# Windowed attention and a hard-swish MLP on one core: an order written by hand for all engines, and transposes moved from TensorE to the DMA engines

## The chip, the cores and the metric

The kernel runs on one core of a Trainium2 chip. A core has TensorE (PE; matmuls and transposes, reading SBUF and writing PSUM), VectorE (DVE), ScalarE (ACT), GpSimd (POOL) and SyncE (SP), which computes nothing and here issues most of the DMAs. Each engine runs its own instructions in order and waits on semaphores for the others. All DMAs share 16 DMA engines. The metric is the device time of one execution in microseconds, the median over several runs; lower is better.

## The reference

```python
q, k, v: (8 batches, 8 heads, 576 positions, 64) f32
scores = q @ k^T / 8;  kept where 0 <= i - j < 64, else -1e9
attn   = softmax(scores) @ v
x      = attn as (4608 tokens, 512)          # token = batch * 576 + position
h      = x @ w_in                            # w_in  (512, 2048)
g      = h * clip(h + 3, 0, 6) / 6
out    = g @ w_out                           # w_out (2048, 512), out (4608, 512) f32
```

The attention is narrow: a query sees 64 keys, so a block of 128 keys meets only 192 queries. The MLP does most of the arithmetic: in tiles of 128 x 128 weights against 512 columns it is 2 x 576 = 1152 matmuls.

## The kernel before

All matmuls take bf16; softmax is done without subtracting the maximum. Two heads together (64 + 64 features) fill 128 partitions and are called a pair; a batch has four pairs. There are nine token blocks T of 512 tokens, which don't coincide with the eight batches of 576.

**Loads.** `load_batch` (lines 67 to 85) brings one batch: q and k in runs of 1536 bytes (six positions of a head, 96 partitions), v in rows of 256 bytes (one position of a head), all issued by SP. The weights come by four plus four DMAs of GpSimd that cast to bf16 on the way (L94, L101). `cast_batch` (L160 to L166) makes bf16 copies; for batch 0 VectorE and ScalarE do it pair by pair, later GpSimd does.

**Attention** for a pair, in `attention`: `tq` (L178) transposes q and k on TensorE, 2 x 6 transposes of 96 x 96, and VectorE and ScalarE copy them out of PSUM, undoing the interleaving. `scores` (L201) computes key-by-query scores in 10 matmuls, ScalarE takes the exponential (L208, L214), VectorE multiplies with the mask (L219). `pv` (L231, L236) multiplies with V in 18 matmuls; a column of ones in V gives the sums, VectorE divides (L242, L245). `xt` (L255) transposes the result on TensorE in five transposes and ScalarE copies it (L260) into xT, features by tokens.

**MLP.** `s1(T)` computes 16 tiles hT (features of w_in by 512 tokens, 4 matmuls each, L280); ScalarE and VectorE make g of them (L285, L286). `s2(T)` multiplies g with w_out into acc, 16 matmuls for each of four groups of 128 tokens (L296); ScalarE copies acc out (L303) and SP stores it (L305).

**Order.** Attention of batch 0 stands alone. After that `weave` runs s1(T) zipped with s2(T-1) and puts the 24 pieces of attention of batch T+1 between them, up to T = 6; T = 7 and 8 have no attention, and s2(8) ends the kernel alone. The framework keeps this order for the engines and places the semaphores. PSUM is given out as one buffer each for transposes, scores, o and acc, and two for hT.

Of the kernel before, what the change touches and what calls it, by code (L numbers as in the profile page):

```python
# [22 lines left out]
def kernel(  # L23
# [15 lines left out]
    assert D == 64 and NG * P == DM and WINDOW == D  # L39
    KB = (S + P - 1) // P  # L40
    SP = KB * P
    R = 6
    NP = S // R
# [3 lines left out]
    assert NTB * TB == NT and NP * R == S  # L47
# [5 lines left out]
    stage = ctx.enter_context(tc.tile_pool(name="stage", bufs=1))  # L53
    nat = ctx.enter_context(tc.tile_pool(name="nat", bufs=2))
    small = ctx.enter_context(tc.tile_pool(name="small", bufs=4))
    opool = ctx.enter_context(tc.tile_pool(name="opool", bufs=2))
    gpool = ctx.enter_context(tc.tile_pool(name="gT", bufs=2))
    t1pool = ctx.enter_context(tc.tile_pool(name="t1", bufs=3))
    osbp = ctx.enter_context(tc.tile_pool(name="osb", bufs=3))
    ps_tr = ctx.enter_context(tc.tile_pool(name="ps_tr", bufs=1, space=PSUM))  # L60
    ps_st = ctx.enter_context(tc.tile_pool(name="ps_st", bufs=1, space=PSUM))
    ps_o = ctx.enter_context(tc.tile_pool(name="ps_o", bufs=1, space=PSUM))
    ps_h = ctx.enter_context(tc.tile_pool(name="ps_h", bufs=2, space=PSUM))
    ps_acc = ctx.enter_context(tc.tile_pool(name="ps_acc", bufs=1, space=PSUM))


    def load_batch(b, by_pair):
        qst = stage.tile([P, H, R * D], F32, name="qst", tag="qst")
        kst = stage.tile([P, H, R * D], F32, name="kst", tag="kst")
        vst = stage.tile([P, KB, H, D], F32, name="vst", tag="vst")  # L70
        step = 2 if by_pair else H
        for h0 in range(0, H, step):
            for dst, src in ((qst, q), (kst, k)):
                nc.sync.dma_start(
                    out=dst[:NP, h0 : h0 + step, :],
                    in_=src[b, h0 : h0 + step].rearrange("h (p j) d -> p h (j d)", j=R),
                )
        for kb in range(KB):
            s0 = kb * P
            ss = min(P, S - s0)  # L80
            nc.sync.dma_start(  # L81
                out=vst[:ss, kb, :, :],
                in_=v[b, :, s0 : s0 + ss, :].rearrange("h s d -> s h d"),
            )
        return qst, kst, vst

    stage0 = load_batch(0, True)


    win16 = consts.tile([P, NG, FF], BF16, name="win16")  # L90
    wout16 = consts.tile([P, NFC, DM], BF16, name="wout16")
    WC = FF // 4
    for i in range(4):
        nc.gpsimd.dma_start(  # L94
            out=win16[:, :, i * WC : (i + 1) * WC],
            in_=moe_w_in[:, i * WC : (i + 1) * WC].rearrange("(g p) f -> p g f", p=P),
        )

    def load_w_out():
        for i in range(0, NFC, 4):  # L100
            nc.gpsimd.dma_start(  # L101
                out=wout16[:, i : i + 4, :],
                in_=moe_w_out[i * P : (i + 4) * P, :].rearrange("(c p) j -> p c j", p=P),
            )


    ident32 = consts.tile([P, P], F32, name="ident32")
    make_identity(nc, ident32)
    ident = consts.tile([P, P], BF16, name="ident")
    nc.vector.tensor_copy(out=ident[:], in_=ident32[:])  # L110
    mask32 = consts.tile([P, QW], F32, name="mask32")
    nc.gpsimd.memset(mask32[:], 1.0)
    nc.gpsimd.affine_select(
        out=mask32[:], in_=mask32[:], pattern=[[1, QW]], compare_op=ISGE,
# [3 lines left out]
        out=mask32[:], in_=mask32[:], pattern=[[-1, QW]], compare_op=ISGE,  # L118
        fill=0.0, base=WINDOW - 1, channel_multiplier=1,
    )  # L120
    mask = consts.tile([P, 2 * KB, QW], BF16, name="mask")
    nc.vector.tensor_copy(
        out=mask[:], in_=mask32[:].unsqueeze(1).to_broadcast([P, 2 * KB, QW])
# [3 lines left out]


    NQT, NPT, NV = 3, 3, 2
    QT_ring, KT_ring, P_ring, V_ring = [], [], [], []  # L130
    for i in range(NQT):
        for ring, n in ((QT_ring, "QT"), (KT_ring, "KT")):
            t = consts.tile([P, SP], BF16, name=f"{n}{i}")
            nc.vector.memset(t[:, S:SP], 0.0)
            ring.append(t)
    for i in range(NPT):
        t = consts.tile([P, 2, KB, 2 * P], BF16, name=f"pT{i}")
        nc.gpsimd.memset(t[:], 0.0)
        P_ring.append(t)
    for i in range(NV):  # L140
        t = consts.tile([P, KB, H, VW], BF16, name=f"V{i}")
        nc.gpsimd.memset(t[:, :, :, D:VW], 1.0)
        nc.gpsimd.memset(t[D:P, KB - 1, :, 0:D], 0.0)
        V_ring.append(t)

    xT = consts.tile([P, NG, NT], BF16, name="xT")


    def cast_batch(b, st, first):
        qst, kst, vst = st  # L150
        qn = nat.tile([P, R, H, D], BF16, name="qn")
        kn = nat.tile([P, R, H, D], BF16, name="kn")
        V = V_ring[b % NV]
        step = 2 if first else H
        for h0 in range(0, H, step):
            for i, (n, s) in enumerate(((qn, qst), (kn, kst))):
                o_ap = n[:NP, :, h0 : h0 + step, :].rearrange("p j h d -> p h j d")
                i_ap = s[:NP, h0 : h0 + step, :].rearrange("p h (j d) -> p h j d", j=R)
                if not first:
                    nc.gpsimd.tensor_copy(out=o_ap, in_=i_ap)  # L160
                elif i == 0:
                    nc.vector.tensor_copy(out=o_ap, in_=i_ap)
                else:
                    nc.scalar.copy(out=o_ap, in_=i_ap)
        nc.gpsimd.tensor_copy(out=V[:, 0 : KB - 1, :, 0:D], in_=vst[:, 0 : KB - 1, :, :])
        nc.gpsimd.tensor_copy(out=V[0:D, KB - 1, :, 0:D], in_=vst[0:D, KB - 1, :, :])  # L166
        return qn, kn, V


    def attention(b, cast):  # L170
        st8 = {}

        def tq(g):
            c = cast()
            for n, (src, ring) in enumerate(((c[0], QT_ring), (c[1], KT_ring))):
                tr = ps_tr.tile([P, 1024], BF16, name="tr")
                for j in range(R):
                    nc.tensor.transpose(  # L178
                        out=tr[:, j * NP : (j + 1) * NP],
                        in_=src[:NP, j, 2 * g : 2 * g + 2, :].rearrange("p h d -> p (h d)"),  # L180
                        identity=ident[:NP, :NP],
                    )
                T = ring[(b * NG + g) % NQT]
                o_ap = T[:, 0:S].rearrange("d (p j) -> d p j", j=R)
                i_ap = tr[:, 0:S].rearrange("d (j p) -> d p j", p=NP)
                if n == 0:
                    nc.vector.tensor_copy(out=o_ap, in_=i_ap)  # L187
                else:
                    nc.scalar.copy(out=o_ap, in_=i_ap)
                yield  # L190

        def scores(g):
            QT, KT = QT_ring[(b * NG + g) % NQT], KT_ring[(b * NG + g) % NQT]
            pT = P_ring[(b * NG + g) % NPT]
            for kbs in ((0, 1), (2, 3, 4)):
                st = ps_st.tile([P, 2, 512], F32, name="st")
                off = 0
                for kb in kbs:
                    w = min(QW, SP - kb * P)
                    for h in range(2):  # L200
                        nc.tensor.matmul(  # L201
                            st[:, h, off : off + w],
                            lhsT=KT[h * D : (h + 1) * D, kb * P : (kb + 1) * P],
                            rhs=QT[h * D : (h + 1) * D, kb * P : kb * P + w],
                            start=True, stop=True,
                        )
                    off += w
                nc.scalar.activation(  # L208
                    out=pT[:, :, kbs[0] : kbs[0] + 2, 0:QW],
                    in_=st[:, :, 0 : 2 * QW].rearrange("p h (k w) -> p h k w", k=2),  # L210
                    func=EXP, scale=scale,
                )
                if len(kbs) == 3:
                    nc.scalar.activation(  # L214
                        out=pT[:, :, 4, 0:P], in_=st[:, :, 2 * QW : 2 * QW + P],
                        func=EXP, scale=scale,
                    )
                yield
            nc.vector.tensor_tensor(  # L219
                out=pT[:, :, :, 0:QW], in0=pT[:, :, :, 0:QW],  # L220
                in1=mask[:].rearrange("p (h k) w -> p h k w", h=2), op=MULT,
            )

        def pv(g):
            V = cast()[2]
            pT = P_ring[(b * NG + g) % NPT]
# [64 lines left out]
    def s2(T):  # L291
        gT = gTs[T]
        for ts in range(TB // P):
            acc = ps_acc.tile([P, DM], F32, name="acc")
            for fc in range(NFC):
# [4 lines left out]
                if fc % 4 == 3 and fc < NFC - 1:  # L300
                    yield
# [81 lines left out]
```

## Time and profile before

| | us |
|---|---|
| median of three runs (375.29, 375.0, 375.18) | 375.18 |
| span of the profiled execution, first to last instruction | 372.6 |
| TensorE busy with matmuls | 333.0 |
| ScalarE / VectorE / GpSimd busy | 214.6 / 194.6 / 74.7 |
| first matmul with w_in | 35.35 |
| the longest group: 512-column matmuls with w_in, 545 recorded | 152.2 |
| the next: 512-column matmuls with w_out, 559 recorded | 146.4 |
| 384 transposes of q and k on TensorE | 29.7 |
| 160 transposes of x on TensorE | 15.5 |

The profile names groups by line of the kernel, engine, operation and tile. Matmuls overlap each other, so the busy time of one is longer than the time by which it delays the next; starts tell more than lengths. A few per cent of the matmuls are not recorded (545 of 576). The DMA share is the busy part of the 16 DMA engines, and can go above 1 where packets overlap. The DMA engines moved 42.34 MB at a mean of 114 GB/s, nearly all loads in the first half.

### The profile page before, as it was taken

How to read it: one execution, taken by the hardware profiler on the slowest of the kernel's cores; microseconds unless marked ns; L12 is line 12 of the kernel's file. 1: busy time of each engine (PE TensorE's matmuls, PEld its weight loads, DVE VectorE, ACT ScalarE, POOL GpSimd, SP SyncE). 2: the span in 40 equal slices, each digit the busy share in tenths (PEclk: the TensorE clock that was granted, in tenths of full speed). 3: DMA queues.
4: the chain of work that ended last, by engine and by line, in shares of the span. 5: the costliest groups of instructions: out<-in, count | busy, mean ns of one | idle time of the engine just before them, and what ended most of it. 6: DMA issues, size and time to landing. Idle time of an engine off the chain costs nothing.

```text
span 372.6 us, 6265 instructions
## 1 busy us (share of the span) xinstructions
PE 333.0 (89%) x2544; PEld 168.6 (45%) x2592; DVE 194.6 (52%) x285; ACT 214.6 (58%) x345; POOL 74.7 (20%) x54
## 2 busy tenths in 40 slices
PE   0156789999999999999999999999999999999985
PEld 0134434555545455455545554555445444444432
DVE  2444438865674567466746665656565643343300
ACT  2353358857666666766676667666766644544411
POOL 8505523544511051005200520000000000000000
PEclk9999999999999999999999999999999999999999
DMA  8999999999999148605760000000000010110111
GB/s 189 248 209 239 196 210 222 218 203 237 199 251 224 42 128 184 157 28 138 173 156 31 28 31 28 30 30 28 30 28 31 29 56 28 45 41 28 57 57 56
DMA packets 59676, 42.34 MB, mean 114 GB/s; under 512 B 38656, under 2 KB 55040, under 8 KB 59648
## 3 DMA queue, kind: packets, MB, share of 16 engines
q1 hardware_dynamic: 55424, 37.76, 43.2%
q0 software_dynamic: 4224, 4.19, 6.8%
q8 instruction: 20, 0.33, 0.4%
q14 instruction: 8, 0.07, 0.1%
HBM read 36.70 MB, written 9.44 MB: 124 GB/s over the span
## 4 chain that ended last, share of the span: by engine, by line
PE 51%; ACT 2%; DVE 2%; DMA 1%; another core or an unknown queue 1%; issue 1%; SPq 1%; ACTq 0%
PE acc L296 23%; PE hT L280 20%; PE st L201 2%; PE tr L178 2%; DMA vst<-in_v_dram 1%; PE o L231 1%; PE tr L255 1%; PE o L236 1%; ACT osb L303 1%; DVE pT_145 L219 1%; ACT pT_145 L208 0%; SPq L81 0%; DVE QT_131 L187 0%; DVE pT_147 L219 0%
## 5 line engine op out<-in xcount | busy, mean ns | idle before, releaser
L280 PE MATMUL hT<-xT,win_110 128*128 128x512 bf16 x545 | 152.2, 386 | 3.7 <-ACT xT L260 1.8
L296 PE MATMUL acc<-wout_111,gT 128*128 128x512 bf16 x559 | 146.4, 379 | 3.7 <-ACT osb L303 3.0
L280 PEld LDWEIGHTS <-win_110 128*128 128x128 bf16 x576 | 52.5, 99 | 58.2 <-issue 4.7
L296 PEld LDWEIGHTS <-gT 128*128 128x128 bf16 x576 | 50.6, 98 | 52.8 <-issue 6.3
L160 POOL CAST qn<-qst 96x3072 bf16<-96x3072 f32 x7 | 19.4, 2778 | 74.4 <-issue 56.9
L303 ACT COPY osb<-acc 128x512 f32<-128x512 f32 x36 | 21.6, 601 | 16.3 <-PE acc L296 12.6
L178 PE MATMUL tr<-ident,qn 96*128 96x96 bf16 x192 | 14.9, 219 | 16.7 <-DVE ident L110 15.8
L245 DVE TENSOR_TENSOR opg<-o,rec 128x640 bf16<-128x640 f32 x32 | 26.4, 825 | 1.1
L260 ACT COPY xT<-tr 128x576 bf16<-128x576 bf16 x32 | 20.6, 642 | 9.0 <-PE tr L255 8.5
L178 PEld LDWEIGHTS <-qn 96*128 96x128 bf16 x192 | 12.8, 105 | 25.2 <-issue 14.0
L208 ACT ACTIVATE pT_147<-st 128x768 bf16<-128x768 f32 x20 | 16.1, 808 | 11.5 <-PE st L201 11.5
L208 ACT ACTIVATE pT_143<-st 128x768 bf16<-128x768 f32 x22 | 17.8, 808 | 7.1 <-PE st L201 7.1
L208 ACT ACTIVATE pT_145<-st 128x768 bf16<-128x768 f32 x22 | 17.7, 806 | 5.5 <-PE st L201 5.5
L160 POOL CAST kn<-kst 96x3072 bf16<-96x3072 f32 x7 | 19.2, 2740 | 6.6 <-DMA kst<-in_k_dram 6.6
L219 DVE TENSOR_TENSOR pT_143<-pT_143,mask 128x1920 bf16<-128x1920 bf16 x11 | 13.2, 1199 | 9.8 <-ACT pT_143 L214 9.8
L219 DVE TENSOR_TENSOR pT_145<-pT_145,mask 128x1920 bf16<-128x1920 bf16 x11 | 13.2, 1196 | 9.5 <-ACT pT_145 L214 9.5
L178 PEld LDWEIGHTS <-kn 96*128 96x128 bf16 x192 | 12.8, 105 | 11.1 <-issue 5.9
L178 PE MATMUL tr<-ident,kn 96*128 96x96 bf16 x192 | 14.8, 219 | 3.0 <-DVE QT_135 L187 1.3
L255 PE MATMUL tr<-ident,opg 128*128 128x128 bf16 x160 | 15.5, 231 | 2.0 <-DVE opg L245 1.2
L219 DVE TENSOR_TENSOR pT_147<-pT_147,mask 128x1920 bf16<-128x1920 bf16 x10 | 12.5, 1253 | 8.5 <-ACT pT_147 L214 8.5
L255 PEld LDWEIGHTS <-opg 128*128 128x128 bf16 x160 | 11.4, 102 | 10.6 <-DVE opg L245 4.4
L242 DVE RECIPROCAL rec<-o 128x10 f32<-128x10 f32 x32 | 6.9, 217 | 10.6 <-PE o L236 10.6
(355 smaller groups left out, 429.7 us busy)
## 6 DMA issues: line engine op xcount, KB each, us to landing
out_dram<-osb SPq DMA_DIRECT2D x36, 256.0 KB, 2.0
vst<-in_v_dram SPq DMA_DIRECT2D x32, 256.0 KB, 7.6
qst<-in_q_dram SPq DMA_DIRECT2D x6, 1152.0 KB, 9.2
kst<-in_k_dram SPq DMA_DIRECT2D x6, 1152.0 KB, 12.8
qst<-in_q_dram SPq DMA_DIRECT2D x8, 288.0 KB, 7.7
kst<-in_k_dram SPq DMA_DIRECT2D x8, 288.0 KB, 8.5
win_110<-in_moe_w_in_dram POOLq DMA_DIRECT2D x4, 512.0 KB, 15.2
wout_111<-in_moe_w_out_dram POOLq DMA_DIRECT2D x4, 512.0 KB, 15.0
```

The source lines that it names most:

```text
L160: nc.gpsimd.tensor_copy(out=o_ap, in_=i_ap)
L178: nc.tensor.transpose(out=tr[:, j * NP : (j + 1) * NP], in_=src[:NP, j, 2 * g : 2 * g + 2, :].rearrange("p h d -> p (h d)"), identity=iden ...
L201: nc.tensor.matmul(st[:, h, off : off + w], lhsT=KT[h * D : (h + 1) * D, kb * P : (kb + 1) * P], rhs=QT[h * D : (h + 1) * D, kb * P : kb * ...
L208: nc.scalar.activation(out=pT[:, :, kbs[0] : kbs[0] + 2, 0:QW], in_=st[:, :, 0 : 2 * QW].rearrange("p h (k w) -> p h k w", k=2), func=EXP, ...
L219: nc.vector.tensor_tensor(out=pT[:, :, :, 0:QW], in0=pT[:, :, :, 0:QW], in1=mask[:].rearrange("p (h k) w -> p h k w", h=2), op=MULT,)
L242: nc.vector.reciprocal(out=rec[:].unsqueeze(3), in_=ov[:, :, :, D:VW])
L245: nc.vector.tensor_tensor(out=opg[:].rearrange("p k h d -> p h k d"), in0=ov[:, :, :, 0:D], in1=rec[:].unsqueeze(3).to_broadcast([P, 2, KB ...
L255: nc.tensor.transpose(out=tr[:, qb * P : (qb + 1) * P], in_=opg[:, qb, :, :].rearrange("p h d -> p (h d)"), identity=ident[:],)
L260: nc.scalar.copy(out=xT[:, g, b * S : (b + 1) * S], in_=tr[:, 0:S])
L280: nc.tensor.matmul(hT[:], lhsT=win16[:, g, fc * P : (fc + 1) * P], rhs=xT[:, g, t0 : t0 + TB], start=(g == 0), stop=(g == NG - 1),)
L296: nc.tensor.matmul(acc[:], lhsT=gT[:, fc, ts * P : (ts + 1) * P], rhs=wout16[:, fc, :], start=(fc == 0), stop=(fc == NFC - 1),)
L303: nc.scalar.copy(out=osb[:], in_=acc[:])
```

## The change

The program is rewritten in one piece. The framework's own ordering is switched off (`manual_schedule`): each engine gets its instructions in the order in which the program writes them, and semaphores are still placed by the framework.

- **Weights** come as f32 by plain DMAs from SP through a staging ring of four buffers (`load_win`, `load_wout`), and GpSimd casts them.
- **Batches 0 and 1** (`load_qk_long`): q and k in runs of 2304 bytes (nine positions), so that two heads fill 128 partitions; one set of nine 128 x 128 transposes on TensorE (`tp_long`) serves two pairs, and the halves are copied out by VectorE and ScalarE. v of these two is issued by ScalarE. x of these two is transposed on TensorE as before.
- **Batches 2 to 7**: q in runs of 1024 bytes (four positions), k and v in rows of 256 bytes, all by SP. GpSimd casts them, and then SP issues DMA transposes from SBUF to SBUF: two for k, two for q per batch (`tk`, `tq`). x is transposed by DMA too, one per pair and block of 128 queries, more where a token block ends inside (`xt_dma`): 20 to 24 per batch. The queries stand in permuted order inside blocks of 64, so the mask and the stores follow that order, and a store of 128 tokens becomes two.
- **Order**: attention 0, s1(0), s2(0) by quarters of w_out (`s2_first`), attention 1 alone; then for T = 1 to 8 s1(T), and s2(T) with attention of batch T+1 in between (scores of pair g after 10g matmuls, pv after 16 + 10g). s1 and s2 are no longer zipped. At the top of each T SP gets the transposes of batch T+1 and then the loads of batch T+2.
- **PSUM**: three buffers of two banks for everything but acc, two for acc. The activation and the product of the MLP take two hT tiles at once (128 x 1024). gT has one buffer instead of two, the last scores of a pair are 64 columns wide instead of 128.

```diff
-    def load_batch(b, by_pair):
...
+    ctx.enter_context(tc.manual_schedule())
+    def load_qk_long(b, gg):
+        st = stage()
+        sv = st[:, 0 : 4 * S].rearrange("p (c a f) -> p c a f", c=2, a=2)
+        for c, src in ((0, q), (1, k)):
+            for a in range(2):
+                h0 = 4 * gg + 2 * a
+                nc.sync.dma_start(
+                    out=sv[:, c, a, :],
+                    in_=src[b, h0 : h0 + 2].rearrange("h (p j) d -> (h p) (j d)", j=J9),
+                )
+        return sv
...
+    qk0 = [load_qk_long(0, 0), load_qk_long(0, 1)]
+    v0 = load_rows(nc.scalar, v, 0)
...
+    def tq(n, t):
+        QT = qkt.tile([P, 4, NG, QJ], BF16, name="QT", tag="QT")
+        o = QT[:].rearrange("d j g p -> d (j g) p")
+        nc.sync.dma_start_transpose(out=o[:, :, 0:P], in_=n[:].rearrange("p j h d -> p (j h d)"))
+        nc.sync.dma_start_transpose(
+            out=o[:, :, P:QJ], in_=t[:].rearrange("p j h d -> p (j h d)")
+        )
+        return QT
+
+    def tk(n):
+        KT = qkt.tile([P, KB, NG, P], BF16, name="KT", tag="KT")
+        nc.gpsimd.memset(KT[:, KB - 1, :, D:P], 0.0)
+        nc.sync.dma_start_transpose(
+            out=KT[:, 0 : KB - 1].rearrange("d k g p -> d (k g) p"),
+            in_=n[:, 0 : KB - 1].rearrange("p k h d -> p (k h d)"),
+        )
+        nc.sync.dma_start_transpose(
+            out=KT[:, KB - 1, :, 0:D], in_=n[0:D, KB - 1].rearrange("p h d -> p (h d)")
+        )
+        return KT
+
+    def xt_dma(b, g, opg):
+        for qb in range(KB):
+            n = P if qb < KB - 1 else D
+            for T, o, f, c in xparts(b, qb * P, n):
+                nc.sync.dma_start_transpose(
+                    out=xtile(T)[:, g, o : o + c], in_=opg[f : f + c, qb, :]
+                )
...
+    def s1(T):
+        gT = gpool.tile([P, NFC, TB], BF16, name="gT", tag="gT")
+        x = xtile(T)
+        for c in range(0, NFC, 2):
+            hT = big()
+            for i in range(2):
+                for g in range(NG):
+                    nc.tensor.matmul(
+                        hT[:, i, :], lhsT=win16[:, g, (c + i) * P : (c + i + 1) * P],
+                        rhs=x[:, g, :], start=(g == 0), stop=(g == NG - 1),
+                    )
...
+            nc.scalar.activation(
+                out=t1[:], in_=hT[:], func=RELU, bias=half[:], scale=1.0 / 6.0
+            )
+            nc.vector.scalar_tensor_tensor(
+                out=gT[:, c : c + 2, :], in0=t1[:], scalar=1.0, in1=hT[:], op0=MIN, op1=MULT,
+            )
...
+    nat_cast(0, 0, qk0[0], (D_, A_, D_, A_))
+    win_st = [load_win(0)]
+    nat_tp(0, 0, 0, (D_, A_))
+    nat_tp(0, 0, 1, (D_, A_))
+    nat_cast(0, 1, qk0[1], (G_, D_, G_, D_))
+    nat_s(0, 0)
...
+    drive(s1(0), {})
+    v1 = load_rows(nc.scalar, v, 1)
...
+    for T in range(1, NTB):
+        b = T + 1
+        side = {}
+        if b < B:
+            cast_perm(b)
+            tr_perm(b)
+            if b + 1 < B:
+                pend[b + 1] = (
+                    load_q4(b + 1), load_rows(nc.sync, k, b + 1), load_rows(nc.sync, v, b + 1)
+                )
+            for g in range(NG):
+                side.setdefault(10 * g, []).append(lambda g=g: perm_s(b, g))
+                side.setdefault(16 + 10 * g, []).append(lambda g=g: perm_pv(b, g))
+        drive(s1(T), {})
+        drive(s2(T), side)
```

## The prediction

> **What bounds the kernel now.** I read the busy shares first, then the stages, then TensorE's own timeline, then the queue of the SyncE sequencer (SP).
>
> The page's first part, and busy time by stage (each row: stretch in us, its length, then busy us and instruction count for each engine, granted clock, DMA share, GB/s):
>
> ```profile
> PE 333.0 (89%) x2544; PEld 168.6 (45%) x2592; DVE 194.6 (52%) x285; ACT 214.6 (58%) x345; POOL 74.7 (20%) x54
> ...
> 0.00:35.30 35.30, 11.20 (x113) 7.97 (x115) 12.72 (x23) 11.80 (x17) 19.10 (x26) 1.00 1.07 221
> 35.30:73.00 37.70, 31.93 (x275) 16.82 (x279) 23.78 (x33) 23.73 (x40) 15.34 (x7) 1.00 1.14 212
> ...
> 258.00:295.00 37.00, 36.54 (x305) 18.63 (x310) 22.17 (x33) 24.52 (x40) 0.00 (x0) 1.00 0.08 30
> 295.00:352.00 57.00, 56.56 (x262) 25.64 (x266) 22.84 (x34) 28.04 (x43) 0.00 (x0) 1.00 0.10 38
> 352.00:372.60 20.60, 14.24 (x63) 6.14 (x63) 0.40 (x1) 2.78 (x5) 0.00 (x0) 1.00 0.17 64
> ```
>
> The kernel has two characters. Until some 75 us the DMA share is above 1 and TensorE is mostly waiting; after that TensorE has no idle time until the last stage. So time can be won at the start by bringing data sooner, and later only by giving TensorE less to do. The clock is 1.00 everywhere.
>
> TensorE's timeline inside a steady stage (start us, length us, line, operation, count), and at the end:
>
> ```profile
> 223.63 0.42 PE L178 MATMUL tr<-ident,qn 96*128 96x96 bf16 x6
> 223.89 1.03 PE L296 MATMUL acc<-wout_111,gT 128*128 128x512 bf16 x4
> ...
> 222.04 0.45 PE L255 MATMUL tr<-ident,opg 128*128 128x128 bf16 x5
> 222.33 0.59 PE L296 MATMUL acc<-wout_111,gT 128*128 128x512 bf16 x2
> ...
> 352.49 3.61 PE L296 MATMUL acc<-wout_111,gT 128*128 128x512 bf16 x16 [0.67 <-ACT osb L303]
> ```
>
> Sixteen 512-column matmuls take 3.61 us, the last of them 0.38, so one follows another in (3.61-0.38)/15 = 0.215 us; 64 of them, half a token block, take 13.8 us. Six q or k transposes delay the matmul behind them by 0.26 us (223.63 to 223.89), five x transposes by 0.29.
>
> SP's timeline, the v loads' issues (min/median/max ns), the store's and q's:
>
> ```profile
> 5.86 17.89 SPq L81 DMA_DIRECT2D vst<-in_v_dram  x5
> ...
> 122.25 9.72 SPq L305 DMA_DIRECT2D out_dram<-osb  x2
> ...
> 150.93 4.25 SPq L81 DMA_DIRECT2D vst<-in_v_dram  x4
> 159.04 9.72 SPq L305 DMA_DIRECT2D out_dram<-osb  x2
> ...
> L81 SPq DMA_DIRECT2D vst<-in_v_dram x40: 373/1082/7316, 5.9 to 190.9; - x40
> ...
> L305 SPq DMA_DIRECT2D out_dram<-osb x36: 332/333/4677, 86.1 to 369.7; - x36
> ...
> L74 SPq DMA_DIRECT2D qst<-in_q_dram x14: 340/450/1080, 0.8 to 171.6; - x14
> ```
>
> Stores of the same place in two stages lie 159.04-122.25 = 36.8 us apart: that is a stage, 128 matmuls (27.6 us) and 9.2 us of attention. A load in 256-byte runs holds the sequencer for as long as its data is moving: 17.89 us for five when the DMA engines are full, about 1.06 us each when they are not.
>
> **The start, until block 1 begins.** Before: first w_in matmul at 35.35 us, and block 0 with batch 1 woven in runs to about 77 us, because batch 1's v is cast only at 53.50 us. After: the order is attention 0, s1(0), s2(0), attention 1, with nothing woven in but two transposes.
> - First transposes at 12 us (before: 15.78, waiting for ident). The q and k of two pairs must land and be cast by VectorE and ScalarE; before, a first, smaller q is cast at 3.94 us. But ScalarE now issues the five v loads ahead of its casts. Nothing held: about 7 us. Held like SP's five: 18. I take 12, the middle, since the queue is ScalarE's own but the engines are full.
> - Attention 0 alone: 16.5 us. Before it runs from 15.78 to 35.35 with a 3.06 us wait for V inside: 19.57-3.06 = 16.5. ScalarE's sum supports it: 2 casts of 1.2 (0.83 x 1.5), 4 half evictions of 0.64, 4 pairs of exponentials of 1.9, 4 x copies of 0.9 are 16 us. s1(0) starts at 28.5.
> - s1(0) and s2(0): 2 x 13.8, to 56. Its cover is the data: 15.5 MB of weights and two batches must be in shortly after. They arrive at 235 GB/s as q and k do in the trace (66 us, so 10 late) or at 385, as a store's 2048-byte rows do in the window 357 to 358 (154 GB/s at a DMA share of 0.40; 40 us, not late). The new runs of 2048 and 2304 bytes on all 128 partitions are nearer the store's, v's are not: I take 2 us late. The casts of the weights go to GpSimd: 8 x 1.89 us (its 128x2048 cast) = 15 us, beside TensorE; GpSimd was busy only 20%. Without that cover each would delay a quarter of w_in by 1.9.
> - Attention 1 alone: 16.5 less the first pair's transposes and casts, which lie in s2(0): 13 us. Block 1 starts at 28.5+27.6+2+13 = 71 us, where before it started at about 77 with s2(0) and its 13.8 us still to do.
>
> **Blocks 1 to 6**, each with one batch. Removed: 48 transposes (8 x 0.26 = 2.1 us) and 20 (4 x 0.29 = 1.2), 3.3 us; with the longer stops at some of them (234.01 to 234.49) up to 4.2; I take 3.7. Attention then costs 5.5. Added: at the change from s1 to s2 the scores of the first pair need a two-bank PSUM buffer that the last but one pair of hT still holds: ScalarE 1.2, VectorE 1.3, less the 1.7 of the last pair's matmuls, 0.9 us. The wait of s1 for the last x transposes: pair 3 is done 18 matmuls (3.9 us) before the end; normalization 1.3, three issues of 0.45 and a landing of 2.0 (the store's) are 4.7, so some 0.6. A stage is 27.6+5.5+1.5 = 34.6, six are 207.6 (before 220.8). Bounds of the stall: 0, or SP's backlog, which follows.
>
> **SP per stage.** This is where the change puts its work, in one queue in program order: 8 stores of 0.33 = 2.7; q, k and v of the next batch, 3.54 MB, held while they move: v's 1.18 MB took 5.3 us (188 to 193), three times that less the last 2.3 us that are queued is 13; four bulk transposes of 1.18 MB in 5 us at 235 GB/s; and 20 to 24 transposes of one x block. No DMA transpose is in the trace. Between the store's 0.33 us and the v load's 1.08 us for an issue, I take q's 0.45: a block of 128 rows of 256 bytes is small, nearest to issues that aren't held. Then SP needs 20.7+22x0.45 = 30.6 us, under 34.6, and hides. It stops hiding at (34.6-20.7)/22 = 0.63 us.
>
> [...]
>
> **The end.** Blocks 7 and 8 without attention, 55.2; the last eviction, store and close 3.6 (369.05 to 372.6). With two acc buffers instead of one the 0.67 us stop before each row of s2(8) goes; its four rows are inside the 55.2.
>
> **Sum.** 71+207.6+55.2+3.6 = 337.4 against the profile's span of 372.6. The median of the runs, 375.18, lies 2.6 above that span: 340.0 us.
>
> **Rivals.**
> - *SP becomes the bound (slower).* For: the sum stands only 4 us under TensorE's, and everything that follows on SP waits in line; before, SP spent 198 us merely waiting for ScalarE's evictions, and could. An issue of 1.08 makes a stage 20.7+23.8 = 44.5, 9.9 above; in the five stages with loads that is 50 us: 390 us. With the bulk transposes at half the rate, 5 more each, about 414. It decides against the change from 0.95 us per issue (5 x (20.7+22c-34.6) = 35). Against: q's issue of 1152 KB takes 0.34 us, whatever the size.
> - *The data comes no sooner.* At 235 GB/s batch 1 lands at 66, ScalarE is held until 18 us, block 1 starts at about 83: 352 us; with some backlog of SP (0.75 us per issue: 2.6 x 5) 365. For: the DMA share is already above 1 in all of the first 73 us, and bytes don't shrink; weights are now written in four bytes. Against: the store's 385 GB/s.
> - *Nothing on TensorE's path changes*, as transposes were hidden behind waits: then only the start is won, 340+6x3.7 = 362. Against: 0.26 us between the rows above, with no idle time around.
>
> **How the numbers follow.** Forecast 331 to 350: 0.42. The other two faster cases, 350 to 373: 0.18. SP as the bound: 0.38, half of it above 400. Within 0.2% (what a measurement of this kernel can tell from none): 0.02. So faster 0.60, same 0.02, slower 0.38. For the range: the low end takes ScalarE unheld (5 us less) and half the stalls away, 331; the high end 410 takes in 390 and nearly the half-rate case. The likeliest case's own range is 331 to 350.
>
> **What would show it.** Right: block 1's first w_in matmul at 66 to 76 us; 34 to 35 us between stages; transposes' issues on SP near 0.45 us and SP waiting at each stage's end. Wrong: SP without a gap from stage to stage, s1 waiting for x from a DMA, scores waiting for QT; or ScalarE's first cast after 16 us. What would make it wrong above all is the price of a DMA transpose, which this trace cannot give.

## The result and the profile after

The changed kernel takes 495.4 us (median of four runs, 495.2 to 495.8) where the kernel before took 375.2 beside it: a ratio of 1.319, with a 95% interval of 1.312 to 1.325. The forecast was 340 us, between 331 and 410. It was wrong in direction.

The page of the changed kernel: busy time by engine, TensorE's granted clock in 40 slices (in tenths of full speed), and the chain that ended last, by engine and by line. (The chain is followed back from the last instruction, at each step to what released it, or to the instruction before it on its engine.) L364 issues the transposes of x, L351 and L355 those of k, L342 and L343 those of q; L91 loads k and v, L405 stores; L380 is s1 and L418 s2.

```profile
PE 334.4 (68%) x2168; PEld 161.1 (33%) x2168; DVE 178.5 (36%) x194; ACT 165.0 (33%) x229; POOL 92.1 (19%) x81
...
PEclk8679995999599856889578985597957889589998
...
PE 42%; SPq 37%; DMA 8%; DVE 6%; ACT 4%; issue 3%; ACTq 0%; DVEq 0%
SPq L364 24%; PE acc L418 17%; PE big L380 16%; SPq L351 4%; SPq L405 2%; DVE p L272 2%; SPq L91 2%; DMA xt<-opg 2%; PE big L258 2%; DMA QT<-qn 2%; DMA st<-in_k_dram 2%; ACT p L261 1%; PE acc L435 1%; PE big L435 1%; DMA st<-in_q_dram 1%
```

TensorE's busy time is what it was (333.0 before), but its share of the span fell from 89% to 68%. SP, which computes nothing, is now on 37% of the chain, and one line of it, L364, the DMA transposes of x, on 24%. The clock, 1.00 everywhere before, is below 0.9 in 24 of the 40 slices.

SP's timeline in one stage (start us, length us, line, operation, count), from one KT transpose to the next (KT and QT are the transposed k and q of a batch):

```profile
195.09 6.00 SPq L351 DMA_TRANSPOSE KT<-kn  x1
201.19 1.19 SPq L355 DMA_TRANSPOSE KT<-kn  x1
202.43 2.04 SPq L342 DMA_TRANSPOSE QT<-qn  x1
204.52 1.59 SPq L343 DMA_TRANSPOSE QT<-qnt  x1
...
207.40 8.41 SPq L91 DMA_DIRECT2D st<-in_k_dram  x5
215.86 6.83 SPq L91 DMA_DIRECT2D st<-in_v_dram  x5
222.79 1.23 SPq L405 DMA_DIRECT2D out_dram<-osb  x2
224.12 13.51 SPq L364 DMA_TRANSPOSE xt<-opg  x10
238.07 1.16 SPq L405 DMA_DIRECT2D out_dram<-osb  x2
239.35 13.36 SPq L364 DMA_TRANSPOSE xt<-opg  x10
252.81 2.80 SPq L405 DMA_DIRECT2D out_dram<-osb  x4
255.72 5.94 SPq L351 DMA_TRANSPOSE KT<-kn  x1
```

There is no gap above 0.5 us in 60.6 us: 10.8 for the bulk transposes of k and q, 16.4 for the loads (q's two short issues are left out above), 26.9 for twenty transposes of x with some waits among them, 5.2 for eight stores. The groups of line 364 say what one costs (min/median/max ns):

```profile
L364 SPq DMA_TRANSPOSE xt<-opg x132: 1104/1227/2046, 106.5 to 433.2; - x132
```

An issue holds SP for 1.23 us, though a block of 128 x 128 bf16 has only 32 KB. A QT transpose in the rows above has sixteen such blocks and holds SP for 2.04 us; the KT transpose, also of sixteen, held it for 6.00 here, though for 1.46 in the first stage. TensorE's timeline of the same stage shows what the x issues do to it (in brackets the wait before the row and what ended it):

```profile
188.86 15.16 PE L380 MATMUL big<-xt,win 128*128 128x512 bf16 x61 [7.05 <-DMA xt<-opg]
207.21 0.88 PE L258 MATMUL big<-QT,KT 64*128 64x192 bf16 x10 [3.19 <-DMA QT<-qn]
208.02 4.45 PE L418 MATMUL acc<-wout,gT 128*128 128x512 bf16 x10
...
229.38 0.38 PE L380 MATMUL big<-xt,win 128*128 128x512 bf16 x1 [1.04 <-DMA xt<-opg]
235.02 0.61 PE L380 MATMUL big<-xt,win 128*128 128x512 bf16 x1 [5.26 <-DMA xt<-opg]
243.88 0.61 PE L380 MATMUL big<-xt,win 128*128 128x512 bf16 x1 [8.24 <-DMA xt<-opg]
250.07 12.26 PE L380 MATMUL big<-xt,win 128*128 128x512 bf16 x47 [5.59 <-DMA xt<-opg]
```

Each of the last four rows starts when the x of one more pair has landed. So the two engines take turns. From one start of s1 to the next, 188.86 to 250.07, the stage is: s1 15.2; a wait for QT 3.2; scores and pv, under SP's loads, 16.9 (207.21 to 224.12); SP's x issues up to the last that this block needs 23.5 (to 247.66); its landing 2.4. That makes 61.2. In the last part TensorE is nearly idle, and so are the DMA engines (stretch, length, busy us and count for PE, PEld, DVE, ACT, POOL, granted clock, DMA share, GB/s):

```profile
207.20:224.00 16.80, 16.79 (x149) 8.53 (x150) 7.71 (x10) 7.79 (x14) 7.24 (x4) 0.82 1.18 209
224.00:237.60 13.60, 5.33 (x35) 2.16 (x31) 1.05 (x2) 1.17 (x2) 2.70 (x3) 0.85 0.19 44
237.60:254.00 16.40, 4.54 (x11) 1.53 (x12) 0.43 (x1) 1.11 (x1) 0.00 (x0) 0.50 0.15 36
```

While SP issues x, the DMA share is 0.15 to 0.19, at some 40 GB/s, against 1.18 during the loads. It is not bytes that are short but issues: VectorE had finished the last pair's x at 225.6, 22 us before the last issue that the block needs was over. The start did improve on before: block 1 begins at 83.2 us with s2(0) done, where before it began at about 77 with 13.8 us of s2(0) still to do.

### The profile page after: what moved, and what is told of

Its sections match the earlier page's. It is cut to its first block, busy times and chain, and to the rows that moved or that the text cites. A ratio compares the mean times of both kernels' runs of the same rounds, so it can differ in the third digit from the quotient of the medians.

```text
span 493.6 us, 5570 instructions
## 1 busy us (share of the span) xinstructions
PE 334.4 (68%) x2168; PEld 161.1 (33%) x2168; DVE 178.5 (36%) x194; ACT 165.0 (33%) x229; POOL 92.1 (19%) x81
## 3 DMA queue, kind: packets, MB, share of 16 engines
q10 hardware_dynamic: 9376, 2.36, 2.9%
## 4 chain that ended last, share of the span: by engine, by line
PE 42%; SPq 37%; DMA 8%; DVE 6%; ACT 4%; issue 3%; ACTq 0%; DVEq 0%
SPq L364 24%; PE acc L418 17%; PE big L380 16%; SPq L351 4%; SPq L405 2%; DVE p L272 2%; SPq L91 2%; DMA xt<-opg 2%; PE big L258 2%; DMA QT<-qn 2%; DMA st<-in_k_dram 2%; ACT p L261 1%; PE acc L435 1%; PE big L435 1%; DMA st<-in_q_dram 1%
## 5 line engine op out<-in xcount | busy, mean ns | idle before, releaser
L380 PE MATMUL big<-xt,win 128*128 128x512 bf16 x576 | 145.3, 413 | 111.0 <-DMA xt<-opg 110.7
L390 DVE SCALAR_TENSOR_TENSOR gT<-t,big 128x1024 bf16<-128x1024 bf16 x72 | 87.9, 1221 | 218.6 <-ACT t L387 218.6
L387 ACT ACTIVATE t<-big,half 128x1024 bf16<-128x1024 f32 x72 | 80.2, 1114 | 179.0 <-PE big L380 177.8
L418 PE MATMUL acc<-wout,gT 128*128 128x512 bf16 x512 | 126.4, 397 | 0.0
L380 PEld LDWEIGHTS <-win 128*128 128x128 bf16 x576 | 59.6, 104 | 195.0 <-issue 90.9
L418 PEld LDWEIGHTS <-gT 128*128 128x128 bf16 x512 | 48.1, 101 | 56.8 <-issue 9.4
L261 ACT ACTIVATE p<-big 128x768 bf16<-128x768 f32 x64 | 48.5, 811 | 43.6 <-PE big L258 43.6
L272 DVE TENSOR_TENSOR p<-p,maskp 128x1920 bf16<-128x1920 bf16 x24 | 30.7, 1281 | 43.3 <-ACT p L267 42.9
L231 ACT COPY osb<-acc 128x512 f32<-128x512 f32 x33 | 19.5, 590 | 57.9 <-PE acc L418 57.8
L233 POOL CAST V<-st 128x2048 bf16<-128x2048 f32 (+1 forms) x16 | 21.6, 1372 | 34.0 <-DMA st<-in_v_dram 24.8
L290 PEld LDWEIGHTS <-p 128*128 128x128 bf16 x320 | 23.1, 105 | 7.2 <-DVE opg L280 1.1
L258 PE MATMUL big<-QT,KT 64*128 64x192 bf16 (+1 forms) x240 | 15.2, 259 | 14.6 <-DMA QT<-qn 11.3
L290 PE MATMUL big<-V,p 128*128 128x65 bf16 x320 | 24.6, 204 | 0.7 <-DVE p L272 0.4
L295 PE MATMUL big<-V,p 128*128 128x65 bf16 x256 | 23.4, 204 | 0.0
L295 PEld LDWEIGHTS <-p 128*128 128x128 bf16 x256 | 20.3, 105 | 0.0
L280 DVE TENSOR_TENSOR opg<-big,rec 128x640 bf16<-128x640 f32 x24 | 19.8, 825 | 1.0
```

The source lines that it names most:

```text
L233: eng.tensor_copy(out=o_ap, in_=i_ap)
L258: nc.tensor.matmul(o, lhsT=lhs(h, kb), rhs=r, start=True, stop=True)
L261: nc.scalar.activation(out=pT[:, :, kbs[0] : kbs[0] + 2, 0:QW], in_=st[:, :, 0 : 2 * QW].rearrange("p h (k w) -> p h k w", k=2), func=EXP, ...
L272: nc.vector.tensor_tensor(out=pf, in0=pf, in1=mask[:].to_broadcast([P, 2 * KB, QW]), op=MULT,)
L280: nc.vector.tensor_tensor(out=opg_ap, in0=ov[:, :, :, 0:D], in1=rec[:].unsqueeze(3).to_broadcast([P, 2, KB, D]), op=MULT,)
L290: nc.tensor.matmul(ob, lhsT=pT[:, h, qb, 0:P], rhs=V[:, qb, heads[h], :], start=True, stop=(qb == 0),)
```

## The experiments

The theory after the result, A: a DMA transpose costs its issuer about 1.2 us per instruction, whatever it moves, and SP's program order puts these issues in series with TensorE. Rivals: the price is that of the bytes or blocks (B), or of other traffic in the DMA engines, or of TensorE's lowered clock.

### x on TensorE, everything else as changed

```diff
-        xt_dma(b, g, opg)
+        s[("o", g)] = opg
...
+    def perm_x(b, g):
...
+        for qb in range(KB):
+            nc.tensor.transpose(
+                out=tf[:, qb * P : (qb + 1) * P], in_=opg[:, qb, :], identity=ident[:],
+            )
+        for T, o, f, n in xparts(b, 0, S):
+            copy(nc.scalar, xtile(T)[:, g, o : o + n], tf[:, f : f + n])
...
+                side.setdefault(24 + 10 * g, []).append(lambda g=g: perm_x(b, g))
```

> x of batches 2 to 7 is transposed on TensorE as for batches 0 and 1, q and k stay DMA transposes. Theory A (each DMA transpose costs SP some 1.25 us per instruction, and x waits in that line): the 132 x issues go, SP is left with 11 us of q and k transposes, 16.6 of loads and 5 of stores per stage, under TensorE's 36; 82 + 6 x 36 + 59 + 2.5 = about 360 us. Theory B (the transposed data is the limit: crossbar or DMA engines, by row): two thirds of the rows stay, so a stage falls from 59 to about 40 to 45, 385 to 415 us. Theory C (TensorE's lower clock is a cause and not an effect): the clock stays near 0.82 and a stage near 45 or more.

Measured: 360.8 us in one run, beside 373.5 for before: theory A had 360, B 385 to 415. SP's timeline of a stage:

```profile
194.70 4.94 SPq L351 DMA_TRANSPOSE KT<-kn  x1
...
220.62 9.05 SPq L405 DMA_DIRECT2D out_dram<-osb  x8
229.79 5.97 SPq L351 DMA_TRANSPOSE KT<-kn  x1
```

A stage is 35.1 us (194.70 to 229.79), where the forecast had 34.6. The bulk transposes, loads and stores all stay on SP, and SP now has time to wait for evictions: eight stores take 9.05 us in place of 5.2, because it stands waiting in that row. This run differs from the changed kernel only in how x is transposed, so the 132 DMA transposes of x cost 134.6 us (495.4 - 360.8), 1.02 each, net of what the transposes cost TensorE instead. The clock came back by itself: in the changed kernel it was 0.80 over the six stages (83.2 to 429.2 us), and here each of the page's slices from 90 us to the last but one is at 0.9 or above, so theory C falls.

### Half as many instructions for the same x

```diff
+    RING = 4 * TB
+    xall = consts.tile([P, NG, RING], BF16, name="xt")
...
-        for qb in range(KB):
...
+            nb = (end - s0) // P if f == 0 else 0
...
+            if nb:
                 nc.sync.dma_start_transpose(
...
+                    out=xall[:, g, o : o + nb * P].rearrange("d (k p) -> d k p", p=P),
+                    in_=opg[:, qb : qb + nb, :].rearrange("p k d -> p (k d)"),
                 )
```

> The same x bytes by DMA transposes, but as many blocks as lie in one piece go in one instruction: 68 instead of 132 in the kernel (8, 20, 8, 8, 8, 16 per batch). The x buffer is a ring of four token blocks instead of three. Theory A: 64 x 1.28 us less on the chain, about 413 us. Theory B: the bytes are the same, 490 to 500 us.

Measured: 421.8 us, where theory A had 413. The groups of the two lines that transpose x: 28 instructions of one to four whole blocks, 16 of them of four, and 40 of half a block:

```profile
L368 SPq DMA_TRANSPOSE xt<-opg x28: 1192/1234/2927, 106.3 to 355.9; - x28
...
L375 SPq DMA_TRANSPOSE xt<-opg x40: 1101/1226/2158, 107.6 to 357.2; - x40
```

The median is 1.234 us for the first, most of which have four blocks, and 1.226 for half a block. Up to four blocks the price is per instruction. 64 instructions fewer won 73.6 us, 1.15 each, nearly their whole issue time: they were on the path. B, which had 490 to 500, falls.

### The loads issued by GpSimd

```diff
-                    load_q4(b + 1), load_rows(nc.sync, k, b + 1), load_rows(nc.sync, v, b + 1)
+                    load_q4(b + 1, nc.gpsimd), load_rows(nc.gpsimd, k, b + 1), load_rows(nc.gpsimd, v, b + 1)
```

> The loads of batches 3 to 7 are issued by GpSimd instead of SP, nothing else. Theory A: x transposes no longer stand behind 16.6 us of loads; they can start about 7.5 us earlier in five stages (at the first normalization), 455 to 465 us. Theory B: the DMA engines carry the same, 490 to 500 us.

Measured: 505.9 us, a miss: 16.4 us a stage were taken off SP, and the kernel became 10.5 us slower. The chain in one stage, and windows of it:

```profile
220.60 5.38 DVE p L272
...
237.18 1.06 SPq L364
...
238.29 17.95 DMA xt<-opg
256.25 1.09 SPq L364
```

```profile
218.00:228.00 10.00, 8.29 (x67) 3.92 (x68) 7.37 (x4) 4.03 (x8) 9.17 (x8) 0.83 0.03 7
...
238.30:256.20 17.90, 1.97 (x9) 0.60 (x7) 0.00 (x0) 0.59 (x1) 5.24 (x5) 0.66 0.85 128
```

GpSimd starts the loads only after its casts, at 226.6 us, and so they run where x is transposed: the DMA share there is 0.85 in place of 0.15. One x transpose then took 17.95 us to land, where one took 2.4 in the changed kernel. SP's rows stretch too: twelve x issues took 21.32 us from 164.23 and 23.54 from 291.40, both in stages with loads, where twelve took 15.1 to 16.5 in the changed kernel. In the changed kernel the loads and x stand one behind the other on SP; taken apart they meet in the DMA engines instead. VectorE's mask multiply took 5.38 us at the first pair, which the next runs take up.

### The loads left out, then the casts too

```diff
-                pend[b + 1] = (
-                    load_q4(b + 1), load_rows(nc.sync, k, b + 1), load_rows(nc.sync, v, b + 1)
-                )
+                pend[b + 1] = (q2, k2, v2)      # first run only
...
-            cast_perm(b)                        # from here on second run only
+            if b == 2:
+                cast_perm(b)
+            else:
+                perm[b] = dict(qn=perm[2]["qn"], kn=perm[2]["kn"], p={})
```

> The changed kernel without the loads of q, k and v for batches 3 to 7: batch 2's staged data are cast again in their place, so the results of those batches are not the reference's; everything else, the 22 DMA transposes of x in a stage too, stays. In the changed kernel's SP timeline the loads take 16.6 us of a stage of 60.6 and stand between the transposes of q and the first transpose of x. If SP's sum alone sets the stage, five stages lose 16.6 each: 495 - 83 = 412 us. Theory A (SP's program order is a chain with TensorE's: x is ready about 8 us before SP has issued the last load, and what then bounds the stage is s1 14 us, scores and pv 7.5, 22 x 1.23 + 8 x 0.54 of issues 31.3, last landing 2.4, in all 52 to 55): 5 x 6 to 9 less, 450 to 465 us, with 1.23 us per x transpose unchanged. Rival (the transposes are slow because the loads' bytes are in the same DMA engines): the issues of x fall well below 1 us each and the time goes under 410.

Measured: 480.9 us, only 14.5 less: a miss in size. GpSimd's and VectorE's timelines of one stage:

```profile
207.52 1.88 POOL L323 CAST qnt<-stq 16x2048 bf16<-16x2048 f32 x1 [52.18 <-DMA QT<-qnt]
209.35 1.88 POOL L331 CAST kn<-st 128x2048 bf16<-128x2048 f32 x1
...
211.75 2.44 POOL L233 CAST V<-st 128x2048 bf16<-128x2048 f32 x2
...
214.40 1.88 POOL L318 CAST qn<-st 128x2048 bf16<-128x2048 f32 x1
```

```profile
209.23 9.13 DVE L272 TENSOR_TENSOR p<-p,maskp 128x1920 bf16<-128x1920 bf16 x2 [3.48 <-ACT p L267]
```

Two mask multiplies took 9.13 us beside casts that follow each other without a pause until 216.3. By the chain the first of them had 8.07. Hence the second run.

> The run without loads (480.9 us) again, now without GpSimd's casts of batches 3 to 7 too: those batches work on batch 2's cast q and k and on the v of batch 2 or 1 that is still in its tile, so their results are not the reference's. In the run without loads GpSimd cast from 207.5 to 216.3 us without a pause, and VectorE's first mask multiply, 1.16 us by itself, took from 209.2 to 217.3. Theory A (the gain of the missing loads was there and the mask multiply beside the casts ate it): the multiply is back at 1.2 us in every stage, the stages come down from 55 to 61 us to 48 to 52, and the time is 440 to 455 us. Rival (something else sets those stages, the 24 transposes of x and the stores by themselves): 470 us or more.

Measured: 472.7 us. The groups of the mask multiply (min/median/max ns), without the loads and without both:

```profile
L272 DVE TENSOR_TENSOR p<-p,maskp x24: 1146/1159/8062, 103.8 to 392.1; 128x1920 bf16<-128x1920 bf16 x24
```

```profile
L272 DVE TENSOR_TENSOR p<-p,maskp x24: 1157/1158/1159, 102.9 to 383.9; 128x1920 bf16<-128x1920 bf16 x24
```

The multiply came back to 1.16 us everywhere, as A said, but that was worth 8.2 us, not 30 or more, and the time ended on the rival's side of 470. SP's timeline shows where the rest is:

```profile
246.01 6.07 SPq L351 DMA_TRANSPOSE KT<-kn  x1
...
265.17 1.12 SPq L405 DMA_DIRECT2D out_dram<-osb  x2
266.86 16.80 SPq L364 DMA_TRANSPOSE xt<-opg  x12
...
285.01 15.92 SPq L364 DMA_TRANSPOSE xt<-opg  x12
301.03 2.81 SPq L405 DMA_DIRECT2D out_dram<-osb  x4
303.96 5.99 SPq L351 DMA_TRANSPOSE KT<-kn  x1
```

This stage is 57.9 us with no load in it, and SP is idle for some 9 of them, from the end of the QT transposes at 257.1 to 266.9 but for two stores, while TensorE computes the scores that x needs. Then 24 issues and the stores take 37 us. Loads and casts together were worth 22.7 us (495.4 - 472.7), 4.5 a stage in five stages, though they were 16.4 us of SP's time: in the changed kernel they lay beside the 16.9 us of scores and pv. Even without any load the x issues, in turn with TensorE, hold the kernel 97 us above before.

The 8.06 us is far longer than any single cast beside it (1.88 us at most), and why the multiply waits across several of them no run shows.

### Half of the x transposes issued by ScalarE

```diff
-                nc.sync.dma_start_transpose(
+                (nc.scalar if g % 2 else nc.sync).dma_start_transpose(
```

> The changed kernel with the x transposes of the second and fourth pair of a batch issued by ScalarE in place of SP; same instructions, same bytes, same order. Theory A1 (the 1.23 us are spent by the engine that issues): SP loses 11 x 1.23 = 13.5 us a stage, ScalarE gains as much (it is busy for 165 us of 494, some 23 of a stage of 59, so it has room), and six stages give up to 81 us back: 415 to 440 us. Theory A2 (the 1.23 us are the spacing of one transposing unit behind all queues): the two queues' issues stretch to about 2.4 us each where they overlap, and the time stays within 485 to 500 us.

Measured: 512.3 us, slower than either theory had. The groups of the two queues:

```profile
L364 SPq DMA_TRANSPOSE xt<-opg x66: 1089/1226/1929, 107.9 to 439.9; - x66
L364 ACTq DMA_TRANSPOSE xt<-opg x66: 1106/1252/2080, 115.3 to 448.9; - x66
```

Where both queues have work they don't overlap: ScalarE issues five from 226.99 to 233.82 us, SP five from 235.82 to 242.05, and in the stage's last stretch the chain goes from one queue to the other through landings of 2.38, 2.25 and 2.20 us. So the run tells nothing of what two overlapping queues would cost; the median of 1.25 us on ScalarE, which issues one at a time, only shows that the price is not SP's own. And ScalarE is held: it stands idle by 10.4 us, behind those waits and issues, before the exponentials of the last pair.

### TensorE kept busy in its wait for q

```diff
         drive(s1(T), {})
+        if b < B:
+            fill = ps_acc.tile([P, 512], F32, name="fill", tag="acc")
+            for i in range(16):
+                nc.tensor.matmul(fill[:], lhsT=zero[:, 0:P], rhs=zero[:], start=True, stop=True)
```

> The changed kernel with 16 more matmuls of zeros on TensorE (their result is not used) between s1 and s2 of a stage, where it waits some 3 us for the transposed q and the clock granted after the wait was 0.50: the ten matmuls of s2 behind it took 4.38 us in place of 2.2, and s1 at the head of a stage starts at 0.50 too. Theory A (the halved clock after a wait lies on the chain of the changed kernel, between the first scores and SP's x transposes): with the wait filled the granted clock there stays at 1, and six stages win 1 to 3 us each: 477 to 489 us. Rival (behind the wait SP is still in the loads, so TensorE's slowness there is hidden): 493 to 497 us, with the higher clock.

Measured: 495.9 us, as the rival had it. The same stretch behind the wait, in the changed kernel and then here:

```profile
207.20:212.40 5.20, 5.19 (x21) 1.97 (x22) 1.16 (x1) 1.68 (x3) 0.00 (x0) 0.50 0.98 247
```

```profile
213.00:217.00 4.00, 3.84 (x34) 2.03 (x35) 1.16 (x1) 2.54 (x5) 0.28 (x1) 1.00 1.19 270
```

The clock went from 0.50 to 1.00, the ten matmuls from 4.45 us to 2.33, and the time didn't move: SP is still in its loads then. The lowered clock at this place is a consequence of the waits, not a cause of the time. The clock of s1 after the wait for x was not tried; s1 took 15.2 us in the stage above and takes 13.8 at full clock, so 1.4 us a stage is an estimate of what that clock cost there.

### No DMA transposes at all

Batches 2 to 7 are treated like 0 and 1: q and k in 2304-byte runs, `nat_tp`, `nat_s`, `nat_pv`, `nat_x`, woven into s2, and stores in whole blocks.

```diff
-            cast_perm(b)
-            tr_perm(b)
+            cast_nat(b)
+            at(0, nat_tp, 0, 0, (D_, A_)); at(3, nat_tp, 0, 1, (D_, A_)); at(8, nat_s, 0)
...
+            at(57, nat_x, 2, A_); at(59, nat_x, 3, A_)
```

> No DMA transpose at all: batches 2 to 7 go as batches 0 and 1 do, q and k in 2304-byte runs, all transposes on TensorE, woven into s2. Theory A: SP has some 12 us of work per stage and TensorE sets the pace, 27.6 + 9.2 = 37 us per stage, 82 + 6 x 37 + 59 + 2.5 = about 366 us, a little behind e1 (TensorE carries 2 us more per stage). Theory B: also about 366, but then well ahead of e1. Theory C: as long as TensorE has no stop, 1.00 clock and 366 too.

Measured: 369.9 us in one run, where about 366 was expected. It is 9.1 us above the run with only x on TensorE, and a stage is 37.0 us (SP's store rows start at 145.94 and 182.91) in place of 35.1. So q and k are better transposed in bulk by DMA here: few instructions, much in each, and they lie largely beside s1. The loads of q and k, the mask, the stores and the places of the pieces of attention changed in this run as well, so the 9.1 us are not shown to be the transposes' alone.

### The start as well

With x on TensorE, what was left of the forecast's gain was the start: block 1 at 83 to 86 us, not 71. Two kernels try it:

```diff
-            52: [lambda: nat_tp(1, 0, 0, (D_, A_))],
...
+            8: [lambda: nat_tp(1, 0, 0, (D_, A_))],
...
+            58: [lambda: nat_s(1, 3)],
...
-    v1 = load_rows(nc.scalar, v, 1)
+    v1 = load_rows(nc.sync, v, 1)
-    nat_cast(1, 0, qk1[0], (G_, G_, D_, D_))
+    nat_cast(1, 0, qk1[0], (G_, G_, G_, G_))
...
-    v0 = load_rows(nc.scalar, v, 0)             # second kernel only
...
+    v0 = load_rows(nc.gpsimd, v, 0)
```

> The kernel of the first experiment (x of batches 2 to 7 transposed on TensorE, 360.8 us) with attention 1 woven into the first s2: transposes at steps 8, 12, 38, 42 of its 64 matmuls, scores at 18, 28, 48, 58; v of batch 1 loaded by SP in place of ScalarE, and the casts of q and k of batch 1 all on GpSimd. In the first experiment s2 of block 0 ends at 65 us and block 1 starts at 83. If the forecast's reading of the start holds (13 us for attention 1 alone, and its inputs there by 56), block 1 starts at 70 to 74 us, and the time is 348 to 353 us; the price per matmul of the woven part stays below the gap it fills. Rival (the casts or v are late, so the woven scores make s2 wait): block 1 starts at 80 or later and the time is 358 to 365.

> The same as the run before it, and v of batch 0 issued by GpSimd in place of ScalarE, whose queue was held by the five issues until 11.3 us, before its first cast at 12.6. If ScalarE's queue is what holds the first transposes at 13.3 us, they come at 10.5 to 11.5, and the time falls by 2 to 4 us against the run before it. Rival (the first bytes of q and k are not there earlier, or GpSimd's issue makes V's cast late, so that pv of pair 0 waits): within 1 us of it, or above.

Measured: 353.4 us (ratio to before 0.943, interval 0.933 to 0.953), and 351.0 (0.932, interval 0.921 to 0.942). Both beat before and the changed kernel: their runs, 351.1 to 356.0 and 347.9 to 353.7, all lie below those of before beside them, 373.6 to 379.9. Against each other the intervals overlap. The first won 7.4 us on the single run with x on TensorE alone, somewhat less than its theory had, with block 1 at 78.5 us rather than 70 to 74. Two rows of TensorE's timeline in the second:

```profile
5.42 0.68 PE L238 MATMUL big<-ident,qkn 128*128 128x128 bf16 x9 [0.57 <-ACT qkn L224]
...
75.99 0.88 PE L379 MATMUL big<-xt,win 128*128 128x512 bf16 x3
```

The first transposes come at 5.4 us in place of 13.3, earlier than the 10.5 to 11.5 expected, so ScalarE's queue was what held them; yet s1(0) started only 1.3 us sooner (33.7 against 35.0) and block 1 2.5. The chain of this kernel goes through the k of the second two pairs, whose issues end at 4.69 us and for which VectorE waits until 16.62, and then through VectorE, which casts it before its first two masks (5.4 us). Block 1 starts at 76.0 us, still not at 71. The page of this kernel:

```profile
PE 310.6 (90%) x2288; PEld 157.8 (46%) x2288; DVE 179.9 (52%) x190; ACT 181.0 (52%) x277; POOL 98.2 (28%) x90
...
PEclk9556999999999999999999999999999999999998
```

TensorE is at 90% again, and the clock is below 0.9 only in the start and in the last slice.

## Why the prediction was wrong

The forecast's span of 337.4 us and the measured 493.6 lie 156.2 apart: 12.2 at the start, 138.4 in the six stages (83.2 to 429.2, against 207.6), 5.6 at the end.

- **The step that failed: "I take q's 0.45"** for the issue of one x transpose. It is 1.23 us, above the 0.95 from which the prediction let SP decide against the change. q's load issue was taken as nearest because a block is small and such issues aren't held. Neither reason held: a transpose's issue cost the same for half a block as for four (1.226 against 1.234), and the 0.34 us "whatever the size" for q's 1152 KB is true of two of these six issues only; the other four took 0.56 to 0.79. Nor does the price go by block: sixteen blocks in one instruction took 2.04 us for QT and 1.46 to 6.00 for KT, so the bulk transposes are cheap by block and only the x ones are not. That bulk transposes move at the loads' 235 GB/s was the author's estimate; a QT transpose of 0.52 MB lands 4.6 us after its issue begins, 113 GB/s, and x moves at 40.
- **The other terms of SP's sum** were all short: bulk transposes 5, measured 10.8; loads 13, measured 16.4; eight stores 2.7, measured 5.2. (The prediction's own working for the loads, three times 5.3 less 2.3, gives 13.6.) Alone they would have hidden: with x on TensorE the stage is 35.1.
- **SP against TensorE as the larger of two sums.** That was a second fault, of structure. The rival "SP becomes the bound" had the mechanism, and 44.5 us a stage at 1.08 per issue; with the measured terms its own sum gives 10.8 + 16.4 + 5.2 + 22 x 1.23 = 59.5, near the 57.7 of the mean stage. But the runs without loads show that a stage doesn't fall with SP's sum: minus 16.4 was worth 2.9 us, and 4.5 with the casts gone too. Transposes of x can't begin before pv of a pair, and the next s1 can't end its first tile before the last pair's x; between these the issues are in series with TensorE. So "SP waiting at each stage's end" would have come only with a short x phase. The rival's upper price of 414, with the bulk transposes at half rate, was still 81 us too low.
- **TensorE's stage, 34.6 us**: right where SP doesn't interfere, 35.1. Its parts, 27.6 and 5.5 and 1.5, were not tested singly; the 1.5 us of stalls were sized for x issues of 0.45, and with x on TensorE its transposes stand in their place, so that the agreement is in part luck.
- **The start.** The prediction has TensorE "mostly waiting" until some 75 us; its second row shows it busy for 31.93 of 37.70 us, so much less was to be won there than in the first 35. First transposes at 12: they came at 13.3. That ScalarE's v loads hold its first cast was right, and taking them away won 8 us there. Attention 0 alone, 16.5: s1(0) starts at 34.3, so 21. s1(0) and s2(0), 29.6 with the late data: 30.5. Attention 1, 13: it was 18.4, with two masks in 4.5 us. Both attentions lacked cover in the forecast for the same thing: it summed ScalarE alone, while the chain of a pair goes through TensorE, ScalarE, VectorE and back, with VectorE's masks up to 2.96 us beside GpSimd's casts. The start still improved, by 7.6 us (83.2 against 77 + 13.8), as the prediction's first part said it would, only by less than the 19.8 forecast.
- **The end, 58.8**: 64.4 from s1(7)'s start at 429.2 to 493.6. s1(7) still waits for x and runs partly at the lower clock (16.0 in place of 13.8, at 0.82), and 6.8 us lie behind the last matmul, where 3.6 were allowed.
- **The data.** The rival that it comes no sooner, at 235 GB/s, was not what happened, though block 1 did start at the 83 us that it names: that is chance. The first two halves of the MLP took 2.9 us more than their matmuls, where 2 were allowed for late data, but no row shows TensorE waiting for data there. The two sets of transposes put between took 1.0, a wait for an eviction 1.0 and one for x 0.2.
- **The chances.** The prediction said that the price of a DMA transpose was what would make it wrong, and that the trace couldn't give it. Between two ends of 0.33 and 1.08, with the decision at 0.95, it gave 0.38 to the slow side; the range's end of 410 needed about the upper row's price and no second fault. Three of its signs of being wrong came as named: SP without a gap, s1 waiting for x from a DMA, scores waiting for QT. The fourth, ScalarE's first cast after 16 us, did not: it came at 12.6.

Not settled: why the bulk KT transpose takes 5.9 to 6.0 us on SP in the last four stages, but 1.46 and 2.98 in the first two (the run without loads or casts has the same, 2.36 and 2.92 and then 6.0 to 6.2, so those are not the reason); and what an x phase with a cheap issue would give, since no run had one.

## What to carry to other kernels

Count DMA transposes by instruction, on the queue that issues them: here 1.2 us each, whether of half a block or of four blocks. They pay where one instruction moves many blocks beside other work (q and k: the kernel with them on TensorE was 9 us slower), and not where results are transposed piece by piece between two matmul phases (x: 135 us worse). Before taking the larger of two engines' sums for a stage, write down which instruction of the one must follow which of the other; what is in series adds. And a queue that is relieved of its transfers lets them run elsewhere: ask beside what (here beside x, one of whose landings went from 2.4 us to 17.95).

## What the runs showed of the hardware that was not expected

- An issue of a DMA transpose of half a block to four blocks takes 1.23 us on SP, and one of a block or less 1.25 on ScalarE. Sixteen blocks in one instruction took 2.04 us for QT, but 1.46 to 6.00 for KT.
- A VectorE multiply of two SBUF inputs, 1.16 us alone, took up to 8.06 beside back-to-back GpSimd casts, and again 1.16 in all 24 cases when these were left out.
- An x transpose that landed in 2.4 us in the changed kernel took 17.95 with loads in the DMA engines at the same time, at a share of 0.85.
- After a wait of 3.2 us TensorE's granted clock was 0.50 and a 512-column matmul took 0.44 us in place of 0.22; with the wait filled it was 1.00. Here that cost nothing.
